# A fused state-space and SwiGLU block with its gradients: doubled matmuls in the opening, another queue for w2, and re-laid output pools

## The chip, the cores and the metric

The kernel runs on one core of one Trainium2 chip. The metric is the device time of one execution in microseconds (us); lower is better. The program names five engines: PE (TensorE, matrix products), DVE (VectorE), ACT (ScalarE), POOL (GpSimd) and SP (SyncE, which here only issues DMAs). Each has its own instruction queue; in the profile a name with a q (SPq, ACTq) is the queue of that engine, where its DMAs are issued.

## The reference

L = 2048 tokens, D = 576 channels, N = 128 states, F = 4608 hidden units, bfloat16 inputs. Cut to what matters:

```python
def _A_ref(u, A_re, A_im, B_re, B_im, C_re, C_im, log_dt, Dskip):
    dt = jnp.exp(log_dt)[:, None]
    logdA = dt * (A_re + 1j * A_im)
    dB = dt * (B_re + 1j * B_im)
    P = jnp.exp(logdA[:, :, None] * l[None, None, :])        # l = 0 .. L-1
    K = jnp.einsum("dn,dnl,dn->dl", C_re + 1j * C_im, P, dB).real
    y = irfft(rfft(K, 2 * L) * rfft(u, 2 * L))[:L]            # causal convolution
    return y + u * Dskip

def _B_ref(x, w1, w3, w2):
    return (silu(x @ w1) * (x @ w3)) @ w2

xn = layernorm(x)
out = x + _A_ref(xn, ...) * silu(_B_ref(xn, w1, w3, w2))
```

The kernel returns `out` and, for a given `grad_out`, the gradients in the twelve arguments of the forward pass (A_u, the parameters of the state space, w1, w3, w2): thirteen outputs.

## The kernel before

One program does forward and backward in stages. Times in brackets are those of the profiled execution.

**Opening (0 to 125 us), `prologue`, L285.** `log_dt` is loaded on ACT's queue (L311, L312) and behind it A_re (L100); the x tiles are loaded on SP's queue (`ln_load`, L163), and POOL's queue copies x and later `grad_out` from DRAM to DRAM into a turned order (`odd_A_u`, `odd_grad_out`). DVE makes rho = A_re * dt, `split3` cuts rho into three bfloat16 pieces `pc`, which are stored to `PCS_dram` and read back in another order as `lhs_r`. `early_exps` (L542) then makes the real part of the powers: 54 tiles `E_k` of 128x1024; each is two matmuls of 48 rows and 512 columns (L558, `lhs_r` against `sel_val`) into a PSUM tile `e_ps` (two of them in turn), one exponential on ACT, and one store to `E_dram` on SP's queue (262 KB; six `E_k` tiles in turn). It is called three times, for 14, 2 and 2 pairs of chunks, three exponentials a pair. `load_rates` (L425) loads B and C on SP's queue behind the second half of the x tiles. Between them stand the layer norm (`ln_stats`, `ln_scale`, and `ln_turn`, L219 and L225: transposes of the normalised x on PE, behind chosen exponentials), the weights `WT` of the state sum (transposes at L398, scaled on ACT), and at the end `early_spectra` (L564): 8 blocks (half h, band m) of 4 steps, each step four matmuls of 288 columns (L578) and one copy to `u_e` (even steps DVE, odd steps ACT), and one store a block to `UH_dram` on SP. The order in the queues comes from priorities (`pre`, `at`) and, where the class `Chain` (L62) is used, from each instruction being put behind the one before it. `next(gate)` starts the loads of the first FFN weights.

**FFN hidden, state-space kernel and convolution (125 to about 600 us).** `ffn_hidden` (L931) runs nine blocks of 512 hidden units; each has eight steps of 256 tokens (PE L987, L995). A step leaves `s_t` (silu), `g_t`, `u_t` and `h_t` in SBUF, three of each in turn; `h_t` goes to `H_dram` on SP's queue (L1010), `g_t` and `u_t` to `G_dram` and `U_dram` on POOL's (L1012). The steps are interleaved with the generation of the state-space kernel (`ssm_kernel`, which reads `E_dram` back and takes sines on ACT) and with the convolution (`ssm_conv`, whose results go to `S_dram` on ACT's queue, L905).

**FFN output rows (591 to 760 us), `ffn_output`, L1015.** For each of 16 tiles of 128 tokens the 36 blocks of `H_dram` are read transposed on SP's queue (L1589) into `hcA`, `hcB` or `hcC`, then multiplied with `w2` (72 matmuls of 288 columns, L1064) and finished by an epilogue that leaves `out` and `go_o`, whose transposes are gathered in `goT`. `w2` comes in nine loads of 576 KB on POOL's queue (L1043): four into `w2a`, five into tiles `w2g16` to `w2g32`. Rows 0 and 1 run side by side, since their last products wait for the last of `w2`. Pools are laid in SBUF as a stack; the order in which they are opened decides which bytes of the stage before and the stage after they share. Here `o_hc` (hcC) is opened first, then `o_gap`, a tile of 2048 bytes a partition that is not used.

**Backward (from 768 us), `backward`, L1444.** `w2` is loaded as `w2r` (L1567) and transposed by DMA into `w2T` (L1589), both on SP's queue; the first products are `ph` (L1652, `w2T` against `goT`). Their tiles lie where the output stage had the tiles opened first. From there on come the gradients of hidden units, weights, convolution, state-space parameters and, from about 1490 us, of the input (L1760).

The DMAs issued by SP and by ACT take eight semaphores in turn; an issue waits until the DMA eight before it in that common order has ended. DMAs of POOL have semaphores of their own.

Of the kernel before, what the change touches and what calls it, by code (L numbers as in the profile page):

```python
# [10 lines left out]
ACT = mybir.ActivationFunctionType  # L11
# [6 lines left out]
P = 128  # L18
# [43 lines left out]
class Chain:  # L62
# [4 lines left out]
    def __getattr__(self, name):  # L67
        fn = getattr(self.eng, name)

        def call(*a, **kw):  # L70
            with self.tc.issue_after(self.prev.ins) if self.prev is not None else nullcontext():
                self.prev = fn(*a, **kw)
            return self.prev
        return call


class K:
# [79 lines left out]
    def ln_load(self, sb):  # L157
# [3 lines left out]
        for b, xt in enumerate(self.xts):  # L161
            rows = xf[4 * b * P:4 * (b + 1) * P, :].rearrange("(i two p) d -> two p i d", two=2, p=P)
            nc.sync.dma_start(out=xt[:, 0:4:2, :], in_=rows[0])  # L163
# [107 lines left out]
    def load_dmat(self, pool, ap2d, name, fill=0.0):  # L271
# [3 lines left out]
        if D < DT * P:  # L275
            nc.vector.memset(tb[:, DT - 1, :], fill)
        nfull = D // P
        if nfull > 0:
            self.dma(tb[:, 0:nfull, :], ap2d[0:nfull * P, :].rearrange("(c p) n -> p c n", p=P))
        rem = D - nfull * P  # L280
        if rem > 0:
            self.dma(tb[0:rem, nfull, :], ap2d[nfull * P:D, :])
        return tb

    def prologue(self, matp, selp, xp, gate):  # L285
# [12 lines left out]
        with pool(name="par_tmp", bufs=1) as tmp, pool(name="par_pc", bufs=2) as pcp, pool(name="sel_tmp", bufs=1) as st, \  # L298
# [34 lines left out]
            self.dma_engines, self._dma_i = [nc.sync, self.S], 0  # L333
            self.split3(tmp, rho, 2)
            self.sy = Chain(self.tc, nc.sync)
# [6 lines left out]
            self.pre(6)  # L342
            self.ln_load_odd(self.sy)
            self.dma_engines, self._dma_i = [self.sy], 0
            self.load_rates(tmp)
            self.A_im = self.load_dmat(tmp, aps["A_A_im"], "A_im", fill=0.0)
# [10 lines left out]
            self.ln_turn(even, tps, (9, 10, 17, 18, 19))  # L357
            self.ln_root(odd, small, last)
            self.ln_scale(odd)
            self.pre(36)  # L360
# [12 lines left out]
            self.dma_engines = [nc.gpsimd]  # L373
            self.split3(tmp, thr, 0)
            self.split3(tmp, th64, 1)
            self.ln_turn(odd, tps, (28, 29, 36, 37, 38))
            self.pre(42)
# [9 lines left out]
            self.dft_signs()  # L387
            self.dft_rows()
            self.build_selectors(st, selp)
            self.early_exps(SELR, LR_, ep, eps, 14, 16)  # L390
            self.pre(68)
# [12 lines left out]
            self.early_exps(SELR, LR_, ep, eps, 16, 18)  # L404
            self.exps_last = self.S.prev
            self.pre(56)
            self.ln_fold()
            self.pre(60)
            self.early_spectra(up, tps, eps)

    def split3(self, tmp, src, q):
# [10 lines left out]
        for (c, p0, n, h, d1) in self.dsplit():  # L422
            self.dma(self.PCS_dram[q].rearrange("k (d h) n -> h d k n", h=2)[h, d1:d1 + n], pc[p0:p0 + n, :, c, :])

    def load_rates(self, pool):  # L425
        aps = self.aps
        self.B_re = self.load_dmat(pool, aps["A_B_re"], "B_re")
        self.B_im = self.load_dmat(pool, aps["A_B_im"], "B_im")
        self.C_re = self.load_dmat(pool, aps["A_C_re"], "C_re")
        self.C_im = self.load_dmat(pool, aps["A_C_im"], "C_im")  # L430
# [92 lines left out]
    def conv_loads(self, after, part):  # L523
# [10 lines left out]
        elif part == 1:  # L534
            nc.gpsimd.dma_start(out=self.odd["grad_out"][:], in_=self.turned(self.aps["grad_out"].flatten_outer_dims()))
# [6 lines left out]
    def early_exps(self, SELR, LR_, ep, ps, p0, p1):  # L542
# [8 lines left out]
        for c2 in range(2 * p0, 2 * p1, 2):  # L551
            for o in range(0, 2 * TW, 1024):
# [3 lines left out]
                for k in range(2):  # L556
# [7 lines left out]
    def early_spectra(self, up, ps, eps):  # L564
        nc, cfg = self.nc, self.cfg
        D, LT, KT, NB = cfg.D, cfg.LT, cfg.KT, cfg.NB
        W = D // 2
        HW = W // 2
        self.UH_dram = self.dram.tile([4, NB, P, 2, KT, HW], BF16, name="UH_dram")
        for h in range(2):  # L570
            for m in range(NB):
                u = up.tile([P, 2, 2, KT, HW], BF16, name="u_e")
                for kt in range(KT):
                    pt = ps.tile([P, 2, 512], FP32, name="t_ps") if kt % 2 == 0 else eps.tile([P, 2, 512], FP32, name="e_ps")
                    for ri in range(2):
                        for i in range(2):
                            with self.tc.issue_after(self.exps[50].ins):
                                nc.tensor.matmul(pt[:, ri, 0:W].rearrange("p (g h d) -> p g h d", g=2, h=2),  # L578
                                                 lhsT=self.cCS[:, ri, i, kt * P:(kt + 1) * P],
                                                 rhs=self.nat4(self.xts[m][:, 2 * ri + i, :])[:, 2 * h:2 * h + 2],  # L580
                                                 start=(i == 0), stop=(i == 1))
                    copy = nc.vector.tensor_copy if kt % 2 == 0 else self.S.copy
                    copy(out=u[:, :, :, kt, :].rearrange("p q r d -> p r q d"),
# [1343 lines left out]
```

## Time and profile before

| what | us |
|---|---|
| median of three runs | 1863.76 |
| lowest and highest run | 1862.98, 1869.3 |
| the profiled execution, its own time | 1845.18 |
| span of the profiled execution | 1843.4 |
| PE busy (share of the span) | 1673.8 (91%) |
| DVE busy | 1356.9 (74%) |
| ACT busy | 923.8 (50%) |
| POOL busy | 343.2 (19%) |

The span reaches from the first to the last instruction; the remaining 1.8 us of the execution's own time lie around it. The profiled execution is 18.6 us shorter than the median of the runs, so a difference read from the trace is to be set against the trace's own time. The page gives the span in forty equal slices of 46 us, the busy share of each in tenths:

```profile
PE   2889999999996899789989999999999977999998
```

The first slice has PE at 2, the next two at 8; the slices around 600 us (6) and 760 to 810 us (7, 8) are the next low ones. Further low ones stand near 1490 us.

### The profile page before, as it was taken

How to read it: one execution, taken by the hardware profiler on the slowest of the kernel's cores; microseconds unless marked ns; L12 is line 12 of the kernel's file. 1: busy time of each engine (PE TensorE's matmuls, PEld its weight loads, DVE VectorE, ACT ScalarE, POOL GpSimd, SP SyncE). 2: the span in 40 equal slices, each digit the busy share in tenths (PEclk: the TensorE clock that was granted, in tenths of full speed). 3: DMA queues.
4: the chain of work that ended last, by engine and by line, in shares of the span. 5: the costliest groups of instructions: out<-in, count | busy, mean ns of one | idle time of the engine just before them, and what ended most of it. 6: DMA issues, size and time to landing. Idle time of an engine off the chain costs nothing. (4 is left out here: it accounts for less than half of the span.)

```text
span 1843.4 us, 38520 instructions
## 1 busy us (share of the span) xinstructions
PE 1673.8 (91%) x15533; PEld 1229.9 (67%) x15533; DVE 1356.9 (74%) x2098; ACT 923.8 (50%) x1653; POOL 343.2 (19%) x561
## 2 busy tenths in 40 slices
PE   2889999999996899789989999999999977999998
PEld 0345555554542677668877878888887865878876
DVE  6658888878590455498596697948999973887666
ACT  4778888886873111275765657655554510000101
POOL 1202222212232111011111111111111044131032
PEclk9989999999998999899999999999999998999999
DMA  8768999877579988757566576678999999999993
GB/s 225 244 221 309 322 313 330 313 264 269 206 250 170 229 200 204 213 169 215 161 195 180 158 216 181 192 222 228 260 273 239 227 214 221 237 230 226 212 220 86
DMA packets 628224, 416.88 MB, mean 226 GB/s; under 512 B 425678, under 2 KB 565902, under 8 KB 623438
## 3 DMA queue, kind: packets, MB, share of 16 engines
q1 hardware_dynamic: 568836, 278.05, 60.8%
q0 software_dynamic: 32784, 110.06, 17.9%
q10 hardware_dynamic: 26426, 26.33, 5.2%
q8 instruction: 121, 1.98, 0.5%
q14 instruction: 57, 0.47, 0.1%
HBM read 135.60 MB, written 190.89 MB: 177 GB/s over the span
## 5 line engine op out<-in xcount | busy, mean ns | idle before, releaser
L1760 PEld LDWEIGHTS <-acts 128*128 128x128 bf16 x2304 | 225.2, 99 | 77.8 <-DMA acts<-GG_dram 11.9
L1712 PEld LDWEIGHTS <-xn_bf 128*128 128x128 bf16 x2304 | 224.7, 98 | 34.4 <-issue 8.3
L1329 DVE TENSOR_TENSOR pr_q<-et_ps,pz 128x1024 f32<-128x1024 f32 x144 | 176.0, 1222 | 21.2 <-PE et_ps L1324 13.4
L987 PEld LDWEIGHTS <-xnT 128*128 128x128 bf16 x1152 | 107.5, 98 | 124.0 <-issue 34.1
L1652 PE MATMUL ph<-w2T,goT 128*128 128x256 bf16 x1440 | 174.7, 276 | 11.6 <-DMA w2T<-w2r 8.5
L1760 PE MATMUL px<-wT,acts 128*128 128x288 bf16 x1408 | 179.1, 286 | 0.4 <-DMA wT<-in_B_w_dram 0.4
L1332 DVE TENSOR_REDUCE S_all<-pr_q 128x32 f32<-128x1024 f32 x144 | 175.3, 1217 | 3.3
L987 PE MATMUL pg<-wmB_w,xnT 128*128 128x512 bf16 x576 | 155.0, 383 | 15.0 <-ACT g_t L1003 15.0
L1652 PEld LDWEIGHTS <-goT 128*128 128x128 bf16 x1440 | 140.9, 99 | 30.4 <-DMA w2T<-w2r 8.8
L1692 PE MATMUL pgw<-go_o,h_n 128*128 128x288 bf16 x1152 | 150.5, 289 | 6.3 <-DVE h_n L1630 5.5
L987 PE MATMUL pu<-wmB_w,xnT 128*128 128x512 bf16 x576 | 154.7, 381 | 0.0
L1712 PE MATMUL pgw<-gu_n,xn_bf 128*128 128x256 bf16 x1152 | 133.9, 274 | 6.1 <-ACT gw L1696 5.9
L1760 PE MATMUL px<-wA,acts 128*128 128x288 bf16 x896 | 120.0, 292 | 19.2 <-DMA acts<-GG_dram 11.4
L1692 PEld LDWEIGHTS <-h_n 128*128 128x128 bf16 x1152 | 113.4, 99 | 35.2 <-DVE h_n L1630 5.7
L1712 PE MATMUL pgw<-gg_n,xn_bf 128*128 128x256 bf16 x1152 | 130.0, 273 | 0.6 <-ACT gw L1714 0.6
L1001 ACT ACTIVATE s_t<-pg 128x512 bf16<-128x512 f32 x144 | 87.5, 607 | 68.6 <-PE pu L995 32.2
L1655 ACT CAST gh<-ph 128x512 bf16<-128x512 f32 x144 | 82.3, 602 | 75.0 <-PE ph L1652 57.4
L1012 POOL DMA_DIRECT2D G_dram<-g_t x72 | 52.2, 725 | 342.8 <-DVE g_t L1005 202.8
L640 ACT ACTIVATE cs_k<-et_ps 128x512 bf16<-128x512 int16 x216 | 111.3, 628 | 0.0
L1008 DVE TENSOR_TENSOR h_t<-s_t,u_t 128x1024 bf16<-128x1024 bf16 x72 | 49.2, 685 | 71.9 <-DMA H_dram<-h_t 42.8
L1714 ACT CAST gw<-pgw 128x256 bf16<-128x256 f32 x144 | 54.0, 375 | 95.1 <-PE pgw L1712 89.8
L1006 ACT CAST u_t<-pu 128x512 bf16<-128x512 f32 x144 | 87.2, 606 | 8.1 <-PE pu L987 8.0
(312 smaller groups left out, 3174.3 us busy)
## 6 DMA issues: line engine op xcount, KB each, us to landing
G_dram<-g_t POOLq DMA_DIRECT2D x72, 256.0 KB, 4.7
H_dram<-h_t SPq DMA_DIRECT2D x72, 256.0 KB, 3.6
U_dram<-u_t POOLq DMA_DIRECT2D x72, 256.0 KB, 4.3
Q_dram<-q_k SPq DMA_DIRECT2D x36, 512.0 KB, 5.1
h_n<-U_dram POOLq DMA_DIRECT2D x18, 1024.0 KB, 8.7
gg_n<-G_dram POOLq DMA_DIRECT2D x18, 1024.0 KB, 6.2
GU_dram<-gu_n SPq DMA_DIRECT2D x36, 512.0 KB, 5.3
GG_dram<-gg_n SPq DMA_DIRECT2D x36, 512.0 KB, 10.0
```

Of the source, the lines that this page charges most:

```text
L640: nc.scalar.activation(out=CS[:, :, o:o + 256], in_=pt[:].bitcast(I16)[:, :, 0::2], func=ACT.Sin, scale=6.283184 / 2 ** 16)
L987: ins = nc.tensor.matmul(pt[:], lhsT=xnT[:, c, ts], rhs=wm[w][:, c, :], start=(q == 0 and c == 0), stop=(q == 1 and c == nfull - 1))
L1001: nc.scalar.activation(out=s_t[:, :, q, :], in_=pgv, func=ACT.Silu)
L1006: nc.scalar.copy(out=u_t[:, :, q, :], in_=puv)
L1329: nc.vector.tensor_tensor(out=pr[:].rearrange("p r k e -> p r (k e)"), in0=T[h][:].rearrange("p k z d a -> p (k z d a)")[:, None].to_broad ...
L1332: nc.vector.tensor_reduce(out=self.S_all[:, :, d0:d0 + 4], in_=pr[:].rearrange("p r k (d a) -> p (r k) d a", d=4), op=ALU.add, axis=AX.X)
L1652: self.pe_last = nc.tensor.matmul(ph[j][:, k, :].rearrange("p (a f) -> p a f", f=P), lhsT=lw, rhs=rh, start=(n == 0), stop=(n == nfull))
L1655: self.sc(lambda: nc.scalar.copy(out=gh[:, j], in_=ph[j][:]))
L1692: self.pe_last = nc.tensor.matmul(pgw[pi_][:, 0:pw], lhsT=hn[:, tt, fl * P:(fl + 1) * P], rhs=go_o[:, tt, po:po + pw], start=(tt == 0), st ...
L1712: self.pe_last = nc.tensor.matmul(pw_[:, 0:FG], lhsT=self.xn_bf[:, tt, c * P:(c + 1) * P], rhs=nat[:, tt, :], start=(tt == 0), stop=(tt == ...
L1714: self.sc(lambda: nc.scalar.copy(out=gw[:, c], in_=pw_[:, 0:FG]))
L1760: self.pe_last = nc.tensor.matmul(px[pi_][:, 0:pw], lhsT=acts[i][:, ai, fi, :], rhs=w[:, po:po + pw], start=(n == 0), stop=(n == len(steps ...
```

## The change

1. **Order of loads.** A_re is loaded first on SP's queue, ahead of the x tiles, which are chained behind it; the rates B, C and A_im go on POOL's queue; the second half of the x tiles follows the read of `lhs_r` directly.
2. **Warm-up and doubled products.** Eighteen matmuls of 128 rows and 512 columns, whose result is not used, stand between the split of rho and the first exponential. All 54 exponentials run in one call. For 30 of them each of the two matmuls is made twice into the same place (the second overwrites the first with the same values); not for the ten beside which the transposes of `ln_turn` stand (numbers 14, 15 and 20 to 27) and not from number 40 on.
3. **Spectra.** `early_spectrum` makes one block. Blocks (0,0) to (0,2) stand beside exponentials 40 to 51 with DVE copies; (0,3), (1,0), (1,1) and (1,2) after the last exponential with ACT copies, with WT between the second and the third; (1,3) with DVE copies. Each block now goes out in four stores of two steps instead of one of four.
4. **Other DMAs of the opening.** The first FFN weights are loaded behind the store of exponential 20; the turned copy of `grad_out` goes on ACT's queue after the last sine so far, in the FFN stage; the third part of the convolution's constants is loaded two chunks later.
5. **w2.** Its nine loads go on ACT's queue, four behind the tenth store of `S_dram`, five behind the last.
6. **Output pools.** `o_gap` is 10240 bytes a partition and is opened first; `o_hc` is opened after `o_h`. The memset of the last rows of `goT` does not wait for the last w2 load.

The added class `Behind` is not used anywhere.

```diff
@@ load_dmat
-        if D < DT * P:
-            nc.vector.memset(tb[:, DT - 1, :], fill)
...
+            (setter or nc.vector).memset(tb[:, DT - 1, :], fill)
             self.dma(tb[0:rem, nfull, :], ap2d[nfull * P:D, :])
+        self.dma(tb[:, 0:nfull, :], ap2d[0:nfull * P, :].rearrange("(c p) n -> p c n", p=P))
@@ prologue
-            self.dma_engines, self._dma_i = [nc.scalar], 0
-            with self.tc.issue_after(ld.ins):
-                self.A_re = self.load_dmat(tmp, aps["A_A_re"], "A_re", fill=-1.0)
+            self.sy = Chain(self.tc, nc.sync)
+            self.dma_engines, self._dma_i = [self.sy], 0
+            self.A_re = self.load_dmat(tmp, aps["A_A_re"], "A_re", fill=-1.0)
...
-            next(gate)
+            pw = eps.tile([P, 1024], FP32, name="e_ps")
+            for k in range(18):
+                nc.tensor.matmul(pw[:, 0:512], lhsT=pc[:, 2, 0, :], rhs=pc[:, 0, 0:4, :], start=True, stop=True)
+            self.ln_load_odd(self.sy)
...
+            self.dma_engines, self._dma_i = [Chain(self.tc, nc.gpsimd)], 0
+            self.A_im = self.load_dmat(tmp, aps["A_A_im"], "A_im", setter=self.V)
+            self.load_rates(tmp)
...
-            self.early_exps(SELR, LR_, ep, eps, 0, 14)
+            turns = {14: 0, 15: 1, 20: 2, 21: 3, 22: 4, 23: 5, 24: 6, 25: 7, 26: 8, 27: 9}
+            self.early_exps(SELR, LR_, ep, eps, 0, 18, turns)
+            self.exps_last = self.S.prev
+            next(gate)
...
+            lead = iter(range(40, 52))
+            for m in range(3):
+                self.early_spectrum(0, m, up, tps, "t_ps", self.V.tensor_copy, [self.exps[next(lead)] for _ in range(4)])
...
+            for h, m in ((0, 3), (1, 0)):
+                self.early_spectrum(h, m, up, eps, "e_ps", self.S.copy, [self.e_last] * 4)
...
-            self.early_spectra(up, tps, eps)
+            for h, m in ((1, 1), (1, 2)):
+                self.early_spectrum(h, m, up, eps, "e_ps", self.S.copy, [self.e_last] * 4)
+            self.early_spectrum(1, 3, up, tps, "t_ps", self.V.tensor_copy, [self.e_last] * 4)
@@ conv_loads
-            nc.gpsimd.dma_start(out=self.odd["grad_out"][:], in_=self.turned(self.aps["grad_out"].flatten_outer_dims()))
+            with self.tc.issue_after(self.sin_last.ins):
+                nc.scalar.dma_start(out=self.odd["grad_out"][:], in_=self.turned(self.aps["grad_out"].flatten_outer_dims()))
@@ early_exps
-                for k in range(2):
+                n = len(self.exps)
+                for k in (0, 1) if n in turns or n >= 40 else (0, 0, 1, 1):
@@ early_spectrum (new; one block)
+        for k0 in range(0, KT, 2):
+            u = up.tile([P, 2, 2, 2, HW], BF16, name="u_e", tag="u" + name)
+            for kt in range(k0, k0 + 2):
+                pt = ps.tile([P, 2, 512], FP32, name=name)
+                for ri in range(2):
+                    for i in range(2):
+                        with self.tc.issue_after(leads[kt].ins):
+                            nc.tensor.matmul(pt[:, ri, 0:W].rearrange("p (g h d) -> p g h d", g=2, h=2),
+                                             lhsT=self.cCS[:, ri, i, kt * P:(kt + 1) * P],
+                                             rhs=self.nat4(self.xts[m][:, 2 * ri + i, :])[:, 2 * h:2 * h + 2],
+                                             start=(i == 0), stop=(i == 1))
+                copy(out=u[:, :, :, kt - k0, :].rearrange("p q r d -> p r q d"),
+                     in_=pt[:, :, 0:W].rearrange("p r (q d) -> p r q d", q=2))
+            for q in range(2):
+                nc.sync.dma_start(out=self.UH_dram[2 * h + q, m, :, :, k0:k0 + 2], in_=u[:, q])
@@ ffn_hidden
-            ld = Chain(self.tc, nc.sync) if fb else self.sy
-            if fb == 1:
-                ld.prev = self.e_stores[30]
+            ld = Chain(self.tc, nc.sync)
+            if fb < 2:
+                ld.prev = self.kg_load if fb else self.e_stores[20]
@@ ffn_output
-        with self.pool(name="o_hc", bufs=1) as hpc, \
-                self.pool(name="o_gap", bufs=1) as gap, \
+        with self.pool(name="o_gap", bufs=1) as gap, \
...
                 self.pool(name="o_h", bufs=1) as hp, \
+                self.pool(name="o_hc", bufs=1) as hpc, \
...
-            gap.tile([P, 1024], BF16, name="o_gap")
+            gap.tile([P, 5120], BF16, name="o_gap")
...
-                ld = nc.gpsimd.dma_start(out=w2g, in_=aps["B_w2"][fi * P:(fi + GRP) * P, :].rearrange("(c p) d -> p c d", p=P))
+                with self.tc.issue_after(self.s_stores[9 if fi < F0 else -1].ins):
+                    nc.scalar.dma_start(out=w2g, in_=aps["B_w2"][fi * P:(fi + GRP) * P, :].rearrange("(c p) d -> p c d", p=P))
...
-            with self.tc.issue_after(ld.ins):
-                nc.gpsimd.memset(goTt[rem:P, :], 0.0)
+            nc.gpsimd.memset(goTt[rem:P, :], 0.0)
```

More of the change, by code (lines that the diff above doesn't have):

```diff
@@ L74, in __getattr__, with __init__, dma_start @@
         return call
+class Behind:
+    def __init__(self, tc, eng, ins):
+        self.tc, self.eng, self.ins = tc, eng, ins
+    def dma_start(self, **kw):
+        with self.tc.issue_after(self.ins.ins):
+            return self.eng.dma_start(**kw)
 class K:
@@ L162, in ln_load @@
             rows = xf[4 * b * P:4 * (b + 1) * P, :].rearrange("(i two p) d -> two p i d", two=2, p=P)
-            nc.sync.dma_start(out=xt[:, 0:4:2, :], in_=rows[0])
+            self.sy.dma_start(out=xt[:, 0:4:2, :], in_=rows[0])
         nc.gpsimd.dma_start(out=self.odd["A_u"][:], in_=self.turned(xf))
@@ L562, in early_exps, with early_spectrum @@
                 self.e_stores.append(nc.sync.dma_start(out=self.E_dram[c2 // 2, :, o:o + 1024], in_=E[:]))
-    def early_spectra(self, up, ps, eps):
+    def early_spectrum(self, h, m, up, ps, name, copy, leads):
         nc, cfg = self.nc, self.cfg
-        D, LT, KT, NB = cfg.D, cfg.LT, cfg.KT, cfg.NB
-        W = D // 2
+        KT, NB = cfg.KT, cfg.NB
+        W = cfg.D // 2
         HW = W // 2
[L569 to L583, printed above, removed]
-                         in_=pt[:, :, 0:W].rearrange("p r (q d) -> p r q d", q=2))
-                nc.sync.dma_start(out=self.UH_dram[2 * h:2 * h + 2, m].rearrange("q p r k d -> p q (r k d)"),
-                                  in_=u[:].rearrange("p q r k d -> p q (r k d)"))
@@ L639, in kgen_chunk @@
             with self.tc.issue_after(self.exps_last.ins):
[L640 removed]
+                self.sin_last = nc.scalar.activation(out=CS[:, :, o:o + 256], in_=pt[:].bitcast(I16)[:, :, 0::2], func=ACT.Sin,
                                      scale=6.283184 / 2 ** 16)
```

67 lines of the change are left out of this document (31 added, 36 removed).

## The prediction

> **What bounds the kernel now.** I read the page's slices first (PE tenths), then the busy time by windows, then the timelines of the stretches where PE is not full. Windows (us; busy PE, PEld, DVE, ACT, POOL with counts; granted clock; DMA share; GB/s):
>
> ```profile
> 59.00:83.00 24.00, 21.86 (x76) 7.51 (x75) 17.23 (x40) 18.50 (x20) 9.98 (x14) 1.00 0.71 240
> ...
> 87.00:105.00 18.00, 14.75 (x40) 5.24 (x40) 14.41 (x35) 14.46 (x20) 0.00 (x0) 0.50 0.63 226
> ...
> 125.00:540.00 415.00, 404.48 (x4389) 220.24 (x4389) 333.12 (x488) 336.07 (x659) 97.81 (x134) 1.00 0.84 286
> 550.00:625.00 75.00, 51.01 (x302) 28.49 (x301) 14.47 (x24) 21.88 (x43) 17.99 (x26) 0.84 1.09 194
> ...
> 758.00:774.00 16.00, 7.47 (x45) 5.23 (x43) 8.44 (x28) 1.59 (x4) 1.59 (x3) 0.68 1.02 268
> ```
>
> From 125 to 540 PE is 97% busy, so time can only be won before 125, at 550–625 (24 us without a matmul) and at 758–774 (8.5). The change touches these three. In the timelines (start, length, engine, line, work, [idle before <- releaser]):
>
> ```profile
> 13.18 0.83 DVE L72 TENSOR_TENSOR rho<-A_re_bf,dt_col 128x640 f32<-128x640 bf16 x1 [8.55 <-DMA A_re_bf<-in_A_A_re_dram]
> ...
> 27.23 1.88 PE L558 MATMUL e_ps<-sel_val,lhs_r 48*128 48x512 bf16 x4 [23.09 <-DMA lhs_r<-PCS_dram]
> ...
> 39.03 1.94 ACT L72 ACTIVATE E_k<-e_ps 128x1024 bf16<-128x1024 f32 x2 [4.56 <-DMA E_dram<-E_k]
> ...
> 84.21 3.77 ACT L72 ACTIVATE E_k<-e_ps 128x1024 bf16<-128x1024 f32 x4 [0.68 <-PE e_ps L558]
> ...
> 86.20 0.59 PE L558 MATMUL e_ps<-sel_val,lhs_r 48*128 48x512 bf16 x2 [0.33 <-ACT E_k L72]
> 87.12 1.92 PE L558 MATMUL e_ps<-sel_val,lhs_r 48*128 48x512 bf16 x4 [0.33 <-ACT E_k L72]
> ...
> 93.08 4.45 ACT L72 ACTIVATE WT<-e_ps 128x576 bf16<-128x576 f32 x8 [0.27 <-PE e_ps L398]
> ...
> 105.78 0.64 ACT L72 CAST u_e<-e_ps 128x576 bf16<-128x576 f32 x1
> ...
> 125.53 1.02 PE L987 MATMUL pg<-wmB_w,xnT 128*128 128x512 bf16 x4
> ...
> 549.27 33.38 SPq L1589 DMA_TRANSPOSE hcA<-H_dram  x1
> ...
> 570.92 0.72 POOL L1012 DMA_DIRECT2D G_dram<-g_t  x1 [11.00 <-DMA w2g<-in_B_w_dram]
> ...
> 579.60 1.86 PE L987 MATMUL pg<-wmB_w,xnT 128*128 128x512 bf16 x4 [13.82 <-ACT g_t L1003]
> ...
> 601.67 6.14 PE L1064 MATMUL po<-w2a,hcB 128*128 128x288 bf16 x32 [6.33 <-DMA hcB<-H_dram]
> ...
> 767.89 5.99 PE L1652 MATMUL ph<-w2T,goT 128*128 128x256 bf16 x30 [8.53 <-DMA w2T<-w2r]
> ```
>
> What to see: the opening is one chain: A_re lands, rho, three-way split, out to PCS_dram and back (17.33 to 27.2), then 54 exponentials until 105.8, then spectra. Four products take 1.92 at 87.12, where the granted clock reads 0.50, and the same at 29.37; one pair takes 0.59 at 86.20, at full clock. So the opening ran at half clock although the window says 1.00 before the first recorded change (83.6). Two products plus hand-over are then 1.07 per exponential; at full clock four exponentials follow each other in 3.77, 0.94 each.
>
> **Opening: the start.** A_re, issued at 1.82 behind log_dt, lands after 11 among x tiles and two 1.15 MB copies, and DVE stands 8.55 for it; the changed order issues it first on SP's queue, and one of the two copies is gone from there. x tiles issued there at 0.73 were in use at 3.81, so A_re can land near 4–6; after the statistics already queued on DVE (0.82 each) rho starts at 6.5 instead of 13.2. Split and round trip keep their 4.1 and 9.9: products from about 20 instead of 27.2, −7. Bounds: −3 (round trip against the x copy) and −9. The rate loads leave SP for POOL's queue; the 4.56 stall at 34.5, E stores queued behind ten rate loads issued at 28.5–36.4, goes: −4.5. What is late next is ScalarE itself.
>
> **Opening: the products.** 30 of 54 are made twice: 60 more matmuls. At full clock (0.21 each in the rows at 83.7) a doubled one costs PE 0.84 and ScalarE 0.94–1.0, so doubling is hidden under ScalarE; at half clock it costs 4 × 0.43 = 1.71 and is not. I take full clock. For it: 18 matmuls of 512 columns and 128 rows stand right ahead, 3.4 us of which is one period of the clock steps here (83.64 to 87.05). Against it: 48-row products at 91% busy (59–83) did not raise the clock, so they count for less than 128-row ones. Counted by rows (0.375) a doubled stretch has 0.84 × 0.375 = 0.31; counted by groups of 32 rows (0.5) it has 0.42. Periods of 128-row matmuls later in the trace dropped the clock at 0.34 (861.9) and kept it at 0.38 (616.1): it lies between. The Trainium skill, "TensorE: Matmul & The Clock Gate", Part 1: The HAM clock gate, has the full rate follow one busy period of some 3.4 us; by busy time alone the clock would stay up here, which the 91% window contradicts.
>
> At full clock the 54 need 54 × 0.97–1.05 on ScalarE = 52–57. Their stores are 54 × 262 KB = 14.2 MB, with x, rates, first weights and the spectra's stores about 20 MB; 240 GB/s at share 0.71 is 338 when full: 59 us. So exponentials run 20 to 79 against 27.2 to 105.8. Twelve of 32 spectrum steps lie beside the last exponentials with their copies on DVE (0.76 each). Afterwards come 16 ScalarE copies (0.60, 9.6), the eight WT scalings (4.45 and some 1 of PE): 15–16, before 19.7 (105.8 to 125.5). First FFN matmul at 95: **−30** (bounds −38 and +27, the second below).
>
> **grad_out's copy** moves from an idle POOL queue at 8 us into the FFN stage on ScalarE's. 1.18 MB read and written is 2.36 MB, 7 us at 338 GB/s. Cover: DMA share 0.84 there, buffers of three. Without cover +7; I take **+2** (0 to +7).
>
> **Into the output rows.** Before, the w2 loads stand on POOL's queue between the stores of G and U: the store at 570.92 waits 11.00 for a w2 load, g_t is not free, PE stands 13.82. On ScalarE's queue after the S stores the loads no longer hold G and U. But DMA issues wait for the eighth before on the same set of hardware queues (SP and ScalarE share it), so the built order puts w2g20 behind hcA and w2g24 behind hcB, on the engine that empties PE's banks; hcC moves ahead of five H stores, which then wait in it. The winnable idle is 13.8 + 6.3 and some 3 of half clock after the pauses, 23; kept is the transpose hcA (33.38, in DMA at a share of 1.31 and 86 GB/s). I take half, **−12** (−18 to +20).
>
> **Into the backward.** The gap tile grows and o_hc moves, so w2r no longer shares bytes with hcC; its loads and w2T's transposes go ahead some 14 rows. The 8.53 and about 2.7 of half clock until 773 are winnable; the first ph products take columns of goT from earlier rows, so row 15's epilogue (still running at 768) covers nothing of it. **−9** (−2 to −11).
>
> Later work meets fuller DMA: gradients start earlier against the same transfers; +2 (0 to +3).
>
> **Sum.** −30 + 2 − 12 − 9 + 2 = −47 on the profiled execution's 1845.2 (span 1843.4 and 1.8 around it): 1798. That execution is 18.6 below the median of the runs, 1863.8, and I subtract from the median: **1817**.
>
> **Rivals.**
> - *Clock lost in plain doubled stretches, regained at the turns* (0.31 against 0.34 speaks for it; a window with 16 transposes, 80.2, raised the clock). All doubled but the four between the turns, 26 at 1.71 instead of 1.03, add 18, half of the twelve beside the spectra at 1.94 another 6: opening −6, total −23: 1841.
> - *ScalarE blocked by w2 loads.* If hcA ends at 583 as before, FFN step 4 waits for it, step 5 for hcB at 597, three steps at 5 each end at 612; the last w2 load goes out ahead of the last, at 607, and if it takes the 24 of the w2 loads at 550 it lands at 631: rows 0 and 1 end near 637, not 617.3: +20 instead of −12, total −15: 1849. Against: the issue order is built, but without G and U behind w2, and with half of w2 loaded earlier, hcA may be shorter.
> - *Slower: the clock never rises.* Place: all 54 exponentials. Warm-up ends near 18, products begin at 20, the pause drops the clock, and nothing raises it. 30 × 2.12 (one pair of releases included, 29.37 to 31.49) + 22 × 1.94 + 2 × 1.07 = 108, so to 128–130; spectra and WT at half clock 22: FFN at 152, +27; with the other four terms (−17) +10: 1874. It decides when the first FFN matmul comes later than 125.5 + 17 + 9 = 152. For: no 48-row window ever raised the clock. Against: the eight turns in a row, 128-row work, should.
> - *Transposes do not count as activity.* Then from the 15th exponential the clock is down: 16 × 1.71 + 22 × 1.94 + 2 × 1.07 = 72 instead of 42, +30, total −17: 1847. This is what the Trainium skill, "TensorE: Matmul & The Clock Gate", Part 4: PE-mode transpose, would have. The 80.2 window, mostly transposes, went up: against.
>
> **How the numbers follow.** Forecast 0.44, partly cold 0.24, ScalarE blocked 0.15, never up 0.13, transposes 0.04. The range reaches from the forecast with the opening's and the transition's better bounds (−19 at most, 1798) into the rival that is slower, 1868; the forecast alone has 1798 to 1832. A difference under 0.5% (9 us) can't be told from none here. Faster: 0.44 + 0.20 of the partly cold + 0.07 of the blocked + 0.03 = 0.74; same: 0.04 + 0.05 + 0.02 + 0.01 = 0.12; slower: 0.11 + 0.03 = 0.14.
>
> **What would show it.** Right: rho near 6.5, products from 20, granted clock 1.00 from about 15 to 80 with E_k about 1.0 apart, first FFN matmul near 95; no wait of PE on g_t over 5 at 550–600; ph starting within 2 of the last output row. Wrong: E_k 1.7–2.1 apart at clock 0.5; ScalarE idle on a w2 issue for over 10 while PE waits on it; first FFN matmul after 120.

## The result, and the profile after

The changed kernel is **slower** by 0.9%: median 1879.5 us (1862.4 to 1898.3, 20 runs) against 1860.7 (1845.2 to 1882.3, 20 runs), ratio 1.0086, 95% interval 1.0057 to 1.0114. The medians are of all runs, and the ratio leaves out slow ones, over 1.5% above the fastest of the same kernel. Forecast was 1817. The profiled execution of the changed kernel has 1868.2 and a span of 1866.4, against 1845.2 and 1843.4: 23.0 more. The trace of before is that of the fastest of its 20 runs, so 23.0 is more than the typical difference (some 16, by the ratio).

The windows of the changed kernel (us; busy PE, PEld, DVE, ACT, POOL with counts; granted clock; DMA share; GB/s):

```profile
17.00:24.00 7.00, 0.33 (x1) 0.13 (x2) 6.56 (x31) 1.78 (x2) 5.37 (x9) 0.82 1.15 154
24.00:48.00 24.00, 24.00 (x58) 8.01 (x56) 14.26 (x54) 13.48 (x14) 0.00 (x0) 0.50 0.54 185
...
758.00:774.00 16.00, 13.17 (x124) 10.51 (x122) 11.27 (x34) 5.54 (x15) 1.59 (x3) 1.00 0.70 203
```

and its timeline at the places that were shown of before:

```profile
6.96 0.81 DVE L72 TENSOR_TENSOR rho<-A_re_bf,dt_col 128x640 f32<-128x640 bf16 x1
...
11.14 5.76 PE L347 MATMUL e_ps<-pc 128*128 128x512 bf16 x18 [7.67 <-DVE pc L72]
23.67 24.92 PE L578 MATMUL e_ps<-sel_val,lhs_r 48*128 48x512 bf16 x58 [6.78 <-DMA lhs_r<-PCS_dram]
...
27.30 1.02 ACT L72 ACTIVATE E_k<-e_ps 128x1024 bf16<-128x1024 f32 x1 [0.69 <-PE e_ps L578]
29.00 1.02 ACT L72 ACTIVATE E_k<-e_ps 128x1024 bf16<-128x1024 f32 x1 [0.68 <-PE e_ps L578]
...
140.97 0.58 PE L1008 MATMUL pg<-wmB_w,xnT 128*128 128x512 bf16 x1 [1.32 <-ACT u_e L72]
...
564.62 6.62 SPq L1610 DMA_TRANSPOSE hcA<-H_dram  x1
...
593.24 0.38 ACTq L1065 DMA_DIRECT2D w2g<-in_B_w_dram  x1
593.71 0.60 ACT L1022 ACTIVATE s_t<-pg 128x512 bf16<-128x512 f32 x1 [14.17 <-DMA hcB<-H_dram]
...
594.84 1.87 PE L1008 MATMUL pg<-wmB_w,xnT 128*128 128x512 bf16 x4 [12.83 <-ACT g_t L1024]
...
764.37 0.71 PE L1673 MATMUL ph<-w2T,goT 128*128 128x256 bf16 x5
```

What to see. rho is 6 earlier, the warm-up ran, and then PE stood 6.78 until `lhs_r` was back. From 24 to 48 PE is busy without a gap, at clock 0.50: 58 products in 24.9 are 0.43 each. ScalarE needs 1.02 for an exponential and waits 0.68 for PE ahead of each, so E_k come 1.71 apart: PE bounds the opening. The first FFN matmul is at 141.0 instead of 125.5. Further on, hcA takes 6.6 instead of 33.4, but ScalarE stands 14.17 behind the issue of a w2 load and PE 12.83 behind ScalarE. ph follows the last output row directly.

Where the time went, by the start or end of the same instructions in both traces:

| mark (us) | before | after | step |
|---|---|---|---|
| first product | 27.2 | 23.7 | −3.6 |
| last exponential ends | 105.8 | 121.0 | +18.8 |
| first FFN matmul | 125.5 | 141.0 | +0.2 |
| rows 0 and 1 end (144 products po) | 617.6 | 622.3 | −10.8 |
| last product po ends | 759.4 | 764.5 | +0.5 |
| first ph | 767.9 | 764.4 | −8.7 |
| 769th product pgw of `go_o` | 1280.3 | 1279.5 | +2.7 |
| end | 1843.4 | 1866.4 | +23.8 |

The last column is each stage's own gain or loss. The opening loses 15.4, the two next changes win 19.0, and up to 1280 the kernels are level; the rest is lost behind 1280, where both run the same program.

### The profile page after: what moved, and what is told of

The parts are those of the page before. It is cut to its first block, busy times and chain, and to the rows that moved or that the text cites. A ratio compares the mean times of both kernels' runs of the same rounds, so it can differ in the third digit from the quotient of the medians.

```text
span 1866.4 us, 38642 instructions
## 1 busy us (share of the span) xinstructions
PE 1710.2 (92%) x15554; PEld 1246.0 (67%) x15611; DVE 1357.5 (73%) x2098; ACT 923.5 (49%) x1652; POOL 339.6 (18%) x555
## 3 DMA queue, kind: packets, MB, share of 16 engines
q0 software_dynamic: 31104, 103.86, 16.9%
## 5 line engine op out<-in xcount | busy, mean ns | idle before, releaser
L1350 DVE TENSOR_TENSOR pr_q<-et_ps,pz 128x1024 f32<-128x1024 f32 x144 | 175.9, 1222 | 27.2 <-PE et_ps L1345 19.3
L1008 PE MATMUL pg<-wmB_w,xnT 128*128 128x512 bf16 x526 | 144.7, 383 | 21.9 <-ACT g_t L1024 13.8
L1733 PE MATMUL pgw<-gu_n,xn_bf 128*128 128x256 bf16 x1152 | 138.7, 279 | 10.4 <-ACT gw L1717 10.2
L1718 POOL DMA_DIRECT2D out_dram<-gw x36 | 20.0, 555 | 401.2 <-ACT gw L1717 357.8
```

Source lines behind the costliest of these rows:

```text
L1008: ins = nc.tensor.matmul(pt[:], lhsT=xnT[:, c, ts], rhs=wm[w][:, c, :], start=(q == 0 and c == 0), stop=(q == 1 and c == nfull - 1))
L1350: nc.vector.tensor_tensor(out=pr[:].rearrange("p r k e -> p r (k e)"), in0=T[h][:].rearrange("p k z d a -> p (k z d a)")[:, None].to_broad ...
L1733: self.pe_last = nc.tensor.matmul(pw_[:, 0:FG], lhsT=self.xn_bf[:, tt, c * P:(c + 1) * P], rhs=nat[:, tt, :], start=(tt == 0), stop=(tt == ...
```

## The experiments

Ratios are against runs of the kernel before on the same chip, with 95% intervals in brackets; a variant has 12 runs (e2_bridge 10, e6_rows128 only 6).

**e1_single: every product made once.**

```diff
-                for k in (0, 1) if n in turns or n >= 40 else (0, 0, 1, 1):
+                for k in (0, 1):
```

> The changed kernel with every product made once (the 18 warm-up matmuls stay). Theory A (the doubled products run at half clock and cost TensorE 1.71 a tile where one pair costs 1.07 with its hand-over): the E_k of the plain stretches 1.07 apart, last exponential at 121 - 30 x 0.64 = 102, first FFN matmul at about 122 instead of 141, total some 19 below the changed kernel, that is near the kernel before or a little under it. Rival B (the stores of E_k or the other DMAs set the pace, the doubles lie under them): last exponential not before 115, total as the changed kernel.

Ratio 0.9995 (0.9955 to 1.0035). Last exponential at 100.9, first FFN matmul at 123.9, both within 2 of theory A: 30 doubled tiles cost 20 at half clock. Rival B falls. Even so the opening is only 1.7 shorter than before, since it runs at half clock like before's.

**e2_bridge: no pause between warm-up and products.**

```diff
-            for k in range(18):
+            for k in range(50):
```

> The changed kernel with 50 warm-up matmuls instead of 18, so that no pause is left between them (they ended at 16.9) and the first product (23.7). Theory A1 (the clock was lost only in the pause; 48-row products count by groups of 32 rows, 0.42, and hold it): granted clock 1.00 from about 15 to the end of the exponentials, E_k about 1.0 apart, last one near 81, first FFN matmul near 101, total about 40 below the changed kernel. Theory A2 (48-row products count by their rows, 0.31, and don't hold it): the clock falls within two periods of 3.41 after the warm-up, E_k again 1.71 apart, last one at 117 to 121, first FFN matmul at 137 to 141, total as the changed kernel.

Ratio 1.0092 (1.0057 to 1.0127), last exponential at 118.3, first FFN matmul at 138.2, as theory A2 had them. Windows of this kernel:

```profile
18.00:24.00 6.00, 5.95 (x29) 2.65 (x27) 5.52 (x27) 0.75 (x1) 4.32 (x7) 1.00 1.21 150
24.00:28.00 4.00, 3.75 (x17) 1.51 (x17) 4.00 (x12) 2.54 (x3) 0.00 (x0) 1.00 1.08 296
30.00:46.00 16.00, 16.00 (x41) 5.43 (x39) 8.24 (x34) 9.81 (x11) 0.00 (x0) 0.50 0.45 172
```

The products begin at full clock at 24.2; the recorded clock is 0.50 from 29.3 on, and then 16.00 of 16 us busy do not bring it back. So the pause was not the cause: matmuls of 48 rows neither hold the clock nor raise it. The period of 3.41 us behind which the clock fell (25.85 to 29.26) holds twelve products of 0.213: by busy time that is 0.75 of it, by rows 0.28, by groups of 32 rows 0.375 (estimates from the rows of the trace). Busy time alone is thus ruled out, since periods of 128-row matmuls at 0.38 kept the clock. Rows and groups are not told apart: 0.375 lies below 0.38 too, and theory A1 had counted on 0.42.

**e3_filler: the extra matmul has 128 rows.** With 50 warm-ups; the real product overwrites the extra one.

```diff
+                    if not (n in turns or n >= 40):
+                        nc.tensor.matmul(pe[:, 512 * k:512 * k + 512], lhsT=self.ident_bf[:], rhs=self.xts[0][:, 0, 0:512],
+                                         start=True, stop=True)
```

> As the one with 50 warm-up matmuls, but in the 30 doubled tiles the extra matmul of each half is one of 128 rows and 512 columns (identity against x) that the real product overwrites. Theory A1 and A2 alike: activity 0.42 + 0.16 or more, clock held at 1.00, E_k about 1.0 apart, last one near 81, first FFN matmul near 101, total about 40 below the changed kernel and some 20 below the kernel before. If the stores or ScalarE set more than 1.0 a tile (rival B): E_k 1.1 to 1.3 apart at full clock, last one at 85 to 95.

Ratio 1.0033 (0.9991 to 1.0074). The clock held (windows 24 to 50 and 50 to 76 both at 1.00), but E_k were 1.28 apart, last one at 89.5: four matmuls, two for each of two alternating operands, took PE 1.28, not 0.86; whether it is the alternating that costs this was not tried. The first FFN matmul was still at 125.9, where 101 was expected, for a reason of the experiment's own:

```profile
73.31 5.44 DVE L72 TENSOR_TENSOR xt<-xn_bf 128x1152 bf16<-128x1152 bf16 x8 [13.25 <-PE e_ps L579]
...
111.02 1.38 PE L418 MATMUL e_ps<-ident_f,Wr 128*128 128x128 f32 x5 [5.07 <-DVE Wr L72]
```

DVE overwrites the x tiles, which the extra matmuls still read, so it stood 13.25, and Wr, behind that in its order, came late. That 128-row matmuls hold the clock is confirmed; the price is the experiment's.

**e4_tail: the kernel before with parts 5 and 6 alone** (the w2 and pool hunks of the change).

> The kernel before with parts 5 and 6 of the change alone (w2 on ScalarE's queue, pools re-laid). Theory A (the transition and the start of the backward are worth what the changed kernel shows between its first FFN matmul and ph: 11 to the end of rows 0 and 1, 19 to the first ph): first FFN matmul 125.5 as before, ph starts near 749 instead of 768, total 10 to 19 below the kernel before. Rival C (what is won there is given back in the gradient stages, where the changed kernel lost 15 between 1320 and 1450 and 9 more behind): ph starts near 749, total 0 to 5 below the kernel before.

Ratio 1.0020 (0.9975 to 1.0065). Rows 0 and 1 end 9.9 earlier and ph starts at 751.4, 16.5 earlier; at the 769th pgw 11.4 are left, and the total shows none of it: rival C.

**e6_rows128: one product of 128 rows.** Rows 48 to 127 of `lhs_r` are zeroed once, so that the sum over them adds nothing; nothing is doubled, 50 warm-ups.

```diff
+            nc.gpsimd.memset(LR_[:], 0.0)
...
-                for k in (0, 1) if n in turns or n >= 40 else (0, 0, 1, 1):
-                                                   lhsT=LR_[0:48, c2 + ch, :],
-                                                   rhs=SELR[0:48, o1:o1 + 512], start=True, stop=True)
+                for k in (0, 1):
...
+                                                   lhsT=LR_[:, c2 + ch, :],
+                                                   rhs=SELR[:, o1:o1 + 512], start=True, stop=True)
```

> The changed kernel with rows 48 to 127 of lhs_r set to zero, so that each product is one matmul of 128 rows with the same result; no product is made twice; 50 warm-up matmuls. Theory A2 (activity is counted by the rows of a matmul): 0.43 of a period at full clock, above the 0.38 that kept the clock, so the granted clock stays 1.00 from about 15 on, E_k about 1.0 apart, last exponential near 82, first FFN matmul 100 to 108 instead of 141, total 33 to 40 below the changed kernel (ratio to the kernel before about 0.988). Rival D (another engine is next: DVE with Wr, the stores on SP): last exponential near 82 but the first FFN matmul after 115.

Ratio **0.9895 (0.9853 to 0.9937)**, of six runs. First FFN matmul at 108.1, last exponential at 87.6 where 82 was expected. The pace is as expected, the start is 5 late. DVE's and POOL's timelines of this kernel, in order of time:

```profile
6.71 0.81 DVE L72 TENSOR_TENSOR rho<-A_re_bf,dt_col 128x640 f32<-128x640 bf16 x1
7.55 4.80 DVE L72 CAST pc<-rho 128x640 bf16<-128x640 f32 x1
...
7.90 3.96 POOL L329 MEMSET lhs_r<- 128x4608 bf16 x1
```

**e7_before_rows: the same zeroing and 128-row products in the kernel before**, nothing else.

> The kernel before with that one edit: rows 48 to 127 of lhs_r zero, each product one matmul of 128 rows, nothing else changed. Theory A2: at half clock such products fill 0.80 of a period, which raised the clock elsewhere in the trace, so the clock rises within the first ten exponentials; E_k 0.95 to 1.0 apart where 1.07 to 1.08 was the pace, the 4.6 stall on the stores behind the rate loads stays; last exponential at 95 to 100 instead of 105.8, first FFN matmul near 117, total 5 to 9 below the kernel before. If the clock doesn't rise: as the kernel before.

Ratio 0.9940 (0.9895 to 0.9985): first FFN matmul at 117.6, last exponential at 97.7, as expected. The first product stands at 29.5 and the recorded clock goes up at 32.9, where in before it stayed down to 83.6; the zeros, and the products over them, are all that differs. This edit of the operand shape alone beats the kernel before, which the whole change does not.

**before_again and after_again: both kernels unchanged, second traces.**

> The kernel before, unchanged, for a second trace. Theory N (the 33 of hcA and the 24 of idle PE at 550 to 625 were one run's slow DMA, which falls elsewhere in another run): hcA takes under 20, rows 0 and 1 end 5 or more earlier against the first FFN matmul than in the first trace, and a slow DMA of 10 or more stands at another place behind 625. Theory A (it is the w2 loads ahead of the stores, in every run): hcA 25 to 40 again, PE waits 10 or more for g_t.

> The changed kernel, unchanged, for a second trace. First exponential to last about 95 again and the clock lost between the warm-up matmuls and the first product. Theory N: the losses behind the first ph matmul (18 between 764 and 1488 in the first trace) fall at other places and sum to another figure, 5 to 35. Theory C (the re-laid pools or the moved queue cost the gradient stages something in every run): the loss stands again between 1320 and 1450.

In the second trace of before hcA took 32.09 and PE waited 12.43 for g_t: that wait belongs to the kernel, theory N falls for it. But the second trace is 3 ahead of the first at the 769th pgw and 29.9 behind it at the end. Around 1350 to 1370 nearly the same instructions run as follows (windows, before_again, then before):

```profile
1350.00:1370.00 20.00, 16.36 (x148) 13.72 (x146) 15.08 (x16) 5.38 (x9) 0.56 (x1) 1.00 1.24 85
```

```profile
1350.00:1370.00 20.00, 18.46 (x172) 15.72 (x173) 19.72 (x23) 8.70 (x15) 2.19 (x4) 1.00 1.11 241
```

The DMA engines are as full (1.24, 1.11) but move 85 GB/s instead of 241. By the packet records of these two windows a packet of 256 bytes takes 175 ns on average instead of 25, and one of 8192 bytes 763 instead of 354: the same sizes take longer, it is not another mix of sizes. Then PE stands:

```profile
1373.95 1.44 PE L1324 MATMUL et_ps<-gz,qT 128*128 128x128 bf16 x12 [7.59 <-DMA gz<-gK_dram]
1384.79 1.87 PE L1712 MATMUL pgw<-gu_n,xn_bf 128*128 128x256 bf16 x8 [9.40 <-ACT gw L1696]
```

The second trace of the changed kernel has 119.3 for the last exponential, 139.8 for the first FFN matmul and an end at 1866.5, all as the first. Behind ph neither theory is borne out whole. The longest wait of PE lies at the same loads (`acts`, 9.7 until 1581 and 9.5 until 1572) and the next ones differ (4.9 until 1398; 8.3 from 1722 on). Theory C's loss stands again, between the products pgw at 1306 and 1412 (16.3 in the first trace, 13.9 in the second, against the first of before), but the second trace of before, without the change, loses 26.7 there. So spells of slow transfers are part of both kernels.

**e8_act_zero: the zeros written by ScalarE**, 46 warm-ups.

```diff
-            nc.gpsimd.memset(LR_[:], 0.0)
+            self.S.mul(out=LR_[:], in_=self.ident_bf[:, None, :].to_broadcast([P, D // 16, N]), mul=0.0)
```

> As e6_rows128, but the zeros of lhs_r are written by ScalarE, which is idle then, instead of POOL, and 46 warm-up matmuls. In e6 DVE's first cast of the split took 4.80 where it took 0.50, for as long as POOL's memset ran (7.9 to 11.9). Theory P (the memset on POOL held DVE up): the cast takes 0.5 again, the split ends at 11, first product at about 24, first FFN matmul at 103 to 105, total 3 to 5 below e6_rows128. If the 4.80 had another cause: split at 15 again, as e6.

The cast took 0.95, the first product came at 23.1, the first FFN matmul at 103.9: theory P. Ratio 0.9938 (0.9895 to 0.9981), so the 4 won at the start are not seen in the total (its interval and e6's overlap). ScalarE's timeline at the start:

```profile
23.77 22.50 ACT L72 ACTIVATE E_k<-e_ps 128x1024 bf16<-128x1024 f32 x24 [5.02 <-PE e_ps L579]
```

24 exponentials in 22.5 without a wait, 0.94 each: this is what the forecast had supposed of the changed kernel. A pair of products of 128 rows takes PE 0.59 at full clock, as a pair of 48 rows did before (86.20), and the clock holds for the first 26 us and mostly in the next (windows of e8_act_zero):

```profile
24.84 0.59 PE L579 MATMUL e_ps<-sel_val,lhs_r 128*128 128x512 bf16 x2 [0.68 <-ACT E_k L72]
```

```profile
24.00:50.00 26.00, 19.75 (x151) 9.78 (x150) 21.03 (x63) 25.00 (x27) 0.00 (x0) 1.00 0.90 314
50.00:76.00 26.00, 17.20 (x73) 7.13 (x72) 21.27 (x39) 20.70 (x22) 5.86 (x8) 0.93 0.82 276
```

This kernel is 41.0 ahead of before at the first ph and 36.6 at the 721st pgw, then it loses 16.6 at one spell. Since it is 36.6 ahead, the same instructions stand in before some 36 later (windows of e8_act_zero and of before, then SP's and PE's rows of e8_act_zero and SP's of before):

```profile
1229.00:1249.00 20.00, 9.94 (x110) 8.70 (x108) 13.06 (x15) 6.19 (x11) 1.52 (x2) 0.88 1.05 97
```

```profile
1265.00:1285.00 20.00, 20.00 (x207) 17.51 (x206) 19.63 (x23) 9.70 (x17) 3.15 (x5) 1.00 1.11 322
```

```profile
1227.19 21.76 SPq L1697 DMA_DIRECT2D GU_dram<-gu_n  x2
...
1253.35 1.01 PE L1346 MATMUL et_ps<-gz,qT 128*128 128x128 bf16 x8 [14.41 <-DMA gz<-gK_dram]
```

```profile
1262.67 2.55 SPq L1675 DMA_DIRECT2D GU_dram<-gu_n  x2
```

The same two issues (the 23rd and 24th of this store) take SP 21.76 and 2.55; the loads of `gz` stand behind them in its queue. Here too packets of the same size take longer in the slow window: 129 ns instead of 25 at 256 bytes, 888 instead of 335 at 8192.

**e5_pools, e10_w2_only, e11_open_only: the parts apart.** Part 6 alone; part 5 alone; e8_act_zero with parts 5 and 6 undone.

> The kernel before with part 6 alone (pools re-laid), w2 still on POOL's queue. Theory A: hcA 30 or more and the wait for g_t as before, but ph starts right behind the last output row: ph first about 8 earlier than before. If the re-laid pools alone cost the gradient stages the 10 that kernels with parts 5 and 6 seem to lose behind 1280: total at the kernel before or some us above it; else 4 to 8 below.

> The kernel before with part 5 alone (w2 on ScalarE's queue), pools as before. Theory A: hcA near 6 instead of 33, ScalarE waits for the issue of a w2 load, PE waits 10 to 14 for g_t all the same, rows 0 and 1 end about 5 to 10 earlier, the 8.5 before ph stays. If the moved queue alone costs the gradient stages 10: total at the kernel before or above it; else 4 to 8 below.

> e8_act_zero with parts 5 and 6 of the change undone: the opening alone, with products of 128 rows. First FFN matmul at 103 to 105, hcA 32 again. Theory C (parts 5 and 6 give back behind 1280 what they win before): total the same as e8_act_zero within 5, about 20 below the kernel before. Theory A (their 11 are kept): 8 to 12 above e8_act_zero.

Ratios 1.0004 (0.9970 to 1.0037), 0.9985 (0.9940 to 1.0031) and 0.9961 (0.9921 to 1.0001). With the pools alone ph starts right behind the output rows, but these end 9 later (768.5) in this trace, so nothing is won. With w2 moved alone hcA takes 6.9, rows 0 and 1 end 12.6 earlier, and the 8 before ph stay, as expected. Some expectations were missed. hcA, with w2 on POOL's queue, takes 32 to 35 in before (both traces), e7 and g1, but 21 in e5 and e11; with w2 moved it takes 5.5 to 7.0 in every trace. In e5 PE waits 4.52 for g_t and 10.77 for hcB. In e10 the wait for g_t does not come at all; PE waits for hcB instead:

```profile
588.67 3.78 PE L1066 MATMUL po<-w2a,hcB 128*128 128x288 bf16 x15 [10.25 <-DMA hcB<-H_dram]
```

e11 is 17.7 ahead at the first ph. Its ratio lies 0.2% above e8's (some 4 us), its median 8 us, and the intervals overlap: neither theory is decided.

**g1, g2, g3, g4: why the gains do not arrive.** The end minus the start of the 769th pgw was 563, 574, 584 and 596 in the traces of kernels whose DMAs of SP and ScalarE take the semaphores as in the kernel before (before, e7, e5, before_again), and 581 to 599 in the others run before g1. So g1 shifts the semaphores by one place in the kernel before, g2 and g3 shift them back, by two and seven DMAs of 32 bytes in the opening:

```diff
+            for k in range(2):
+                nc.sync.dma_start(out=spare[:, 16 * k:16 * k + 16], in_=aps["A_log_dt"][0:16].rearrange("(o p) -> o p", o=1))
```

g4 is e8_act_zero with 145 warm-ups.

> The kernel before with one DMA of 32 bytes more on the queue of SP in the opening, which shifts the semaphore that each later DMA of SP and ScalarE takes by one of eight. Theory L (the 10 that seem lost behind 1280 come with that shift, which all kernels with any of parts 1 to 5 have, and the kernel before, its re-laid pools alone and its 128-row products alone don't): to 1280 as before, total 8 to 12 above the kernel before. Theory T (they come with arriving earlier, against transfers that set the end): as the kernel before, within 4.

> e8_act_zero with two such DMAs more, so that the gradient stages take their semaphores as in the kernel before. Theory L: total 8 to 12 below e8_act_zero, ratio to the kernel before 0.984 to 0.989. Theory T: as e8_act_zero, 0.994.

> e4_tail (parts 5 and 6 alone) with seven such DMAs more, the shift zero again. Theory L: the 11 that it is ahead at 1270 are kept, total about 10 below the kernel before. Theory T: as e4_tail, within 5 of the kernel before.

> e8_act_zero with 145 warm-up matmuls instead of 46, so that the first product comes about 21 later (99 at 0.213) and all behind it. If the stages behind 1280 don't care when they begin: total 15 to 21 above e8_act_zero, ratio about 1.004. Theory T (what is won before 1280 is lost behind it, to transfers that set the end): total 0 to 10 above e8_act_zero.

Ratios: g1 1.0024 (0.9980 to 1.0068); g2 0.9920 (0.9882 to 0.9957) beside e8's 0.9938; g3 0.9967 (0.9924 to 1.0010) beside e4's 1.0020; g4 0.9996 (0.9957 to 1.0035). All three shifts go the way of theory L, by 0.2 to 0.5%, each inside its interval; the stage took 591, 601 and 579 in their traces. g4 lost about 11 of the 21 against e8, between the two theories. None is decided: the spread of the stage is larger than what was looked for.

The traces narrow it down. Counting all products pgw, each of the other 17 traces keeps its lead or lag against the first trace of before within 2.1 us from the 751st (926.8 in before) to the 2401st (1236.1). Up to the 3751st (1458.5) each of them then loses 2.6 to 31.6. So the loss begins in the same stretch in every trace; there the DMA share of the changed kernel rises to 1.06 (1300 to 1350) and 1.10 (1350 to 1400), from 0.45 to 0.73 between 900 and 1250. The four traces that come to it more than 20 ahead (e6, e8, e11, g2) lose 20.1 to 31.6 in it, 27 in the mean, the other 13 lose 2.6 to 25.0, 12 in the mean. The five others that take the semaphores as in the first (before_again, e5, e7, g2, g3) lose 2.6 to 25.1, 14 in the mean; the other twelve lose 3.0 to 31.6, 17 in the mean. This points to theory T rather than L, but it compares single traces with that of the fastest run, and does not show it.

## Why the prediction was wrong

- **The step that failed: "I take full clock"** for the doubled products: the opening was forecast at −30 and measured at +15.4. The forecast weighed 0.31 of activity (by rows) against 0.42 (by groups of 32 rows), with 0.34 that dropped the clock and 0.38 that kept it, and took the favourable count. The runs showed that products of 48 rows do not hold the clock, also where they come in at full clock (e2), so that a doubled product cost 0.43 a matmul and not 0.21. With 128 rows and not one doubled product e6 and e8 kept it for most of the exponentials, at two matmuls a tile, and e7 raised it by that edit alone. Even by groups the 0.42 was too high: 0.375 in the period of e2 that decided. The row of before that the forecast had against it (21.86 of 24 us busy, and half clock) ruled out busy time alone; it could not tell rows from groups. The rule by busy time in the Trainium skill, "TensorE: Matmul & The Clock Gate", Part 1: The HAM clock gate, has the full rate follow one busy period of some 3.4 us. The forecast rightly set this aside for that row, and the trace of e2 disagrees with it too: 0.75 of a period was busy ahead of the fall.
- **The rival that came true** was "the clock never rises", chance 0.13: the clock was down from 21.5 to 113.6, for nearly all of the exponentials. They took 95 from first to last, where it had 108, with 2.12 for the doubled tile instead of the measured 1.71. Its total, 1874, came near 1879.5 partly by luck: its opening was some 12 too slow, and it had only +2 for the later work. What the forecast held against it, the eight turns in a row, did not raise the clock: their periods (59 to 72.6) are wholly busy, but 0.65 to 0.73 counted by rows (an estimate from the trace's rows), and behind 0.73 (66.6) the clock did not rise in before either; it rose behind 0.82, at 80.2 in before and at 110.2 in the changed kernel. The period at 80.2 in before is 0.72 transposes and 0.28 products of 48 rows, which alone never raised the clock: transposes do count, and the fourth rival is not borne out.
- **The pause.** Warm-up ended at 16.9, as the rival had it, and the clock fell at 21.5. The round trip took 12.6 (stores issued at 11.1, first product at 23.7), not 9.9, so the start won 3.6, not 7. In e2, without the pause, the first FFN matmul came 2.8 earlier (138.2): the pause was not what lost the clock.
- **rho at 6.5**: right (6.96). **The stall behind the rate loads**: gone, right.
- **Behind the last exponential** 15 to 16 were forecast, 20.0 measured; in e8, at its better clock, 21.2 (82.7 to 103.9), since ScalarE's copies wait for PE and for the stores of `u_e`. This term was 4 to 6 too small in both.
- **grad_out's copy +2**: nothing seen; from first to last FFN matmul e11, which has it and the old w2 loads, takes 463.1, before 465.2.
- **Into the output rows −12**: right in size (−10.8; between the second traces −11.3), half right in mechanism, so in part by luck. G and U no longer wait for w2, and hcA fell from 33 to 6, which the forecast had kept. But the wait on ScalarE behind hcB, told as a rival, is there too (14.17), and PE still stands 12.83 for g_t, where the forecast had 13.82 as the largest part of what could be won. What went is the wait for hcB (6.33) and 10 us at half clock (23.9 before, 13.65 after, between 568 and 606). The rival's hcA of 34 did not come, so its price didn't either.
- **Into the backward −9**: right (−8.7), and the pools are the cause: the wait ahead of ph stays with w2 moved alone (7.7 in e10) and goes with the pools alone (e5).
- **Later work +2** is the second term that failed: mis-sized. The first pair of traces has +26.5 behind ph; by the ratio (16 slower, and 3.5 ahead at ph) it is some 19, an estimate. Of the 62 between forecast and result some 45 are the opening and most of the rest is this. Even with the clock held, e8 brings 41 to the first ph and some 11 to the total (0.62% of 1863). The forecast's −49 up to ph was nearly reached there, and the total would still have come out some 35 above the forecast (e8's median is 1852.6).
- **The base.** The forecast read its waits from the fastest run and took its sum off the median. The trace of before has 563 from its 769th pgw on, that of before_again 596. A gain ahead of this stage arrived whole, by the ratios, only where it was small: e7 is 6.0 ahead at the 769th pgw and some 11 at the end, g3 6.8 and 6; but e4 has 11.4 and none, e8 20.0 and some 11, e6 33.2 and some 20. Why is **open**: spells of slow DMA are shown, their dependence on the order of semaphores or on the time of arrival is not.

## What to carry to other kernels

A matmul of few rows counts for less in what holds the clock, whether strictly by its rows or not. Repeating a short-contraction matmul bought nothing here and cost its full time at half clock (20 us in e1), while padding its contraction with zero rows cost PE no time (0.59 a pair either way) and held the clock for most of the stretch. A warm-up is worth only what follows it: ask what share of a period the work behind it fills, counted by rows. And take two traces before a gain ahead of a DMA-filled stage is priced as a gain of the whole: here the unchanged kernel took 563 and 596 from one mark to the end, and its variants up to 601.

The versions that beat both kernels have 128-row products and no doubles: the changed kernel in its two forms with 0.9895 and 0.9938, 0.9920 with two small DMAs more, and the kernel before with that edit alone with 0.9940. These intervals overlap, so it is not shown that the rest of the change adds anything.

## What the runs showed of the hardware that was not expected

- A window wholly busy with 48-row matmuls (24.00 of 24.00 us, the changed kernel) stays at clock 0.50; the same products with 128 rows, 19.75 of 26.00 us busy with other work between (e8), stay at 1.00, and at 0.93 in the next 26 us.
- POOL's memset of 128x4608 (3.96) held a DVE cast of 128x640 for as long: 4.80 (e6) instead of 0.95 without it (e8).
- Four 512-column matmuls on two alternating stationary operands took 1.28 at full clock (e3), not 4 x 0.21; the cause is not shown.
- DMA engines can be full at a third of the rate: share 1.24 at 85 GB/s and 1.11 at 241 over the same 20 us of the same program, since packets of the same size take longer (175 ns instead of 25 at 256 bytes).
